# Selective attention and a gated FFN in one kernel: k's DMA transposes write the matmul operands directly, and the seven-product down projection also serves token tile 1

## The chip, the core and the metric

The kernel runs on one core of one Trainium2 chip. TensorE (PE) multiplies matrices, VectorE (DVE), ScalarE (ACT) and GpSimd (POOL) work on elements, and SyncE (SP) here only issues DMAs. The engines have their own instruction streams, run in program order each, and wait for one another by semaphores. The metric is the device time in microseconds (us); the time before is the median of three runs, 375.34 us (374.61 to 375.9).

## The reference

```python
scores = (q @ k.T) / sqrt(64)                      # 8 batches x 8 heads, 576 x 576, head size 64
cum    = cumsum(maximum(s, 0))
scores = where(causal, -1e9, scores + minimum(-(cum_i - cum_j), 0))
attn   = softmax(scores) @ v                       # -> x, 4608 tokens x 512
g, val = x @ w_gate, x @ w_val                     # 512 -> 1536
out    = (silu(g) * val) @ w_out                   # 1536 -> 512, float32
```

## The kernel before

**Attention.** The 64 heads (called kk, batch-major) go in 16 groups hb of four heads. For each head `score_piece` (line 338) makes the causal half of the transposed scores in four chunks ci = 0 to 3: each takes a PSUM bank, PE multiplies (line 359), ACT takes the exponential into `pt` (line 369) and the bank is free again. POOL masks the diagonal blocks of chunks 0 and 3 (lines 374, 379). `av_piece` (line 386) multiplies by v and a column of ones (line 396), `av_out` (line 404) divides by the sum on DVE (lines 412, 413). There are eight PSUM banks, handed out in the order in which they were given back, so a new use of a bank waits for whoever read it last.

**The operand tiles.** `KQ[hb % 2][r]` (line 91) serves heads 2r and 2r+1 of a group. It has 128 rows and two planes, 0 for q and 1 for k. Rows 64r to 64r+63 hold the 64 features, transposed, of the two heads side by side (2 x 576 = 1152 columns, `NR * S`). The first four rows of the other half hold the bias (parts of the cumulative sums in bf16, made once in `HL`), the rest of that half zeros, so that one 128-row matmul gives q.k plus bias. `aug` (line 178) writes the bias rows of a group with four DMAs from POOL's queue (line 183).

**How q and k get there.** `load_qk` brings 576 KB each for a group into `raw` (line 140), `cast_one` makes bf16. Groups 0 to 4 are transposed on PE. Groups 5 to 15 (`NPE = 5`) go through DRAM: `scratch` (line 258) writes them out, `transposes` (line 267) issues one DMA transpose each for k and q into a 128 x 1152 tile `pk` or `pq`, whose rows are the two heads pairs' features one above the other, and `split` (line 272) copies each half, 64 x 1152, to its `KQ` tile on DVE (line 274): four copies a group. `pk` and `pq` have one buffer each.

**What sets the order.** `attn_items` (line 547) is a generator that emits heads in order; after every chunk it calls `side(h, step, ci)` (line 467), where h is the group in work, step the head in it. `side` is a timetable by hand:

- `load_qk(h + 3)` at (0,1), on SP;
- for group h + 2: casts on ACT early in the group, `scratch` at (2,0), `transposes` at (3,0) (group 6: (3,0) and (3,3)), all DMAs on SP;
- for group h + 1: `aug` at (0,1) on POOL; `split` of k and of q appended to a list `later` at ci = 1 of step 0 and step 1 (groups 5 to 7: steps 1 and 2). Group 5 has its scratch and transposes here, at (0,1) and (0,3).

SP's queue also carries the loads of v and `x_in` (line 434): finished heads go in pairs from POOL (`x_out`, line 430) to a DRAM scratch `xs`, and SP transposes them into the FFN's input `XT` (line 437), which it can do only when `xs` has landed.

**The FFN.** Nine tiles of 512 tokens. `gate_value` (line 644) makes 12 pairs of 128 x 512 products (line 629), tanh on ACT (line 650) and two DVE instructions (lines 652, 663) for each. Then comes the down projection. `down_plain` (line 678) is 48 matmuls of 512 columns (line 686). `down_seven` (line 713) splits the product in 2 x 2 blocks and makes it from seven block products m1 to m7 of 12 matmuls of 256 columns each, 84 in all (line 735). It needs sums of the activations (`su`, lines 670, 671; differences in place, line 672), sums and differences of the weights made once (`weight_op`, line 603: six sums into `WS`, four differences in place in `WO`), and some additions of the outputs (lines 774, 794, 800, 852). Tiles from `FIRST7 = 2` on use `down_seven`, tiles 0 and 1 `down_plain`.

**The interleaving.** The main loop (line 1003) runs through the FFN's items of each tile (about one unit of cost per 512-column quadruple) and calls `pump` to emit attention up to a position, so that both share PE; attention is about four heads and a tile ahead. After each item it may call `do_later(1)`: in the gate stage after every fourth item (in tile 1 every second), in the down stage after every item. That is where the copies enter DVE's stream. All that is left in `later` is emitted at step 0 of the next group.

Of the kernel before, what the change touches and what calls it, by code (L numbers as in the profile page):

```python
# [13 lines left out]
BF16 = mybir.dt.bfloat16  # L14
# [5 lines left out]
def kernel(  # L20
# [11 lines left out]
    nc = tc.nc  # L32
    PSUM = bass.MemoryType.PSUM

    B, H, S, D = q.shape
# [7 lines left out]
    NR = HB // 2  # L43
# [20 lines left out]
    def pt_col(tj, bi):  # L64
# [6 lines left out]
    cp = ctx.enter_context(tc.tile_pool(name="cp", bufs=2))  # L71
# [8 lines left out]
    NPE = 5  # L80
    XB = 2
    KS = {i: dram.tile([NR * S, 128], BF16, name=f"ks{i}") for i in range(NPE, NHB)}
# [3 lines left out]
    QS = {i: dram.tile([NR * S, 128], BF16, name=f"qs{i}") for i in range(NPE, NHB)}  # L86
# [4 lines left out]
    KQ = [  # L91
        [const.tile([128, 2, NR * S + 64], BF16, name=f"kq{e}{i}") for e in range(2)]
        for i in range(2)
    ]
# [9 lines left out]
    first = first_sbuf.enter_context(tc.tile_pool(name="first", bufs=1))  # L104
# [5 lines left out]
    with tc.manual_schedule():  # L110
        loaded = {}
        SRC = {"q": (q, 0), "k": (k, 1)}
# [13 lines left out]
        def give(b):  # L126
            clock[0] += 1
            released[b] = clock[0]
# [18 lines left out]
        def load_qk(hb):  # L147
            load_one(hb, "k")
            load_one(hb, "q")

        def load_v(b, cs, eng=nc.sync):
            if 0 in cs:
                loaded["v", b] = raw.tile([128, NCH, H, D], FP32, tag="rawv", bufs=1, name="rawv")
            t = loaded["v", b]
            for c in cs:
                n = 128 if c < 4 else TAIL
                eng.dma_start(
                    t[0:n, c, :, :],
                    v[b, :, c * 128 : c * 128 + n, :].rearrange("h p d -> p h d"),
                )  # L160

        def cast_v(b, c, eng):
            n = 128 if c < 4 else TAIL
            dst, src_t = VT[b % 2][0:n, c, :, 0:D], loaded["v", b][0:n, c, :, :]
            if eng is nc.scalar:
                nc.scalar.copy(dst, src_t)
            else:
                eng.tensor_copy(dst, src_t)  # L168
# [89 lines left out]
        def scratch(hb):  # L258
            for name, SC in (("k", KS), ("q", QS)):
                nc.sync.dma_start(  # L260
                    SC[hb].rearrange("(x j) c -> x (j c)", j=J),
                    cts[name, hb].rearrange("x j r d -> x (j r d)"),
                )

        prs = {}

        def transposes(hb):
            for name, SC in (("k", KS), ("q", QS)):
                prs[name, hb] = cp.tile([128, NR * S], BF16, tag="p" + name, bufs=1, name="p" + name)
                nc.sync.dma_start_transpose(prs[name, hb], SC[hb])  # L270

        def split(hb, name, r):
            kq = SRC[name][1]
            nc.vector.tensor_copy(
                KQ[hb % 2][r][64 * r : 64 * r + 64, kq, 0 : NR * S],
                prs[name, hb][64 * r : 64 * r + 64, :],
            )

        tps = {}
# [175 lines left out]
        later = []  # L455

        def do_later(n):
            while n > 0 and later:
                f, *args = later.pop(0)
                f(*args)  # L460
                n -= 1
# [5 lines left out]
        def side(h, step, ci):  # L467
            bh = HB * h + step
            for c in V1_AT.get((bh, ci), ()):
                cast_v(1, c, nc.gpsimd)  # L470
            if bh == H + 4 and ci == 3:
                load_v(2, range(5))
            if h == 4 and (step, ci) in ((0, 1), (2, 1)):
                load_qk(6 + step // 2)
            if h >= 5 and h + 3 < NHB and (step, ci) == (0, 1):
                load_qk(h + 3)
            hb = h + 1
            if NPE <= hb < NHB:
                late = hb == NPE
                if late and (step, ci) == (0, 1):  # L480
                    scratch(hb)
                if late and (step, ci) == (0, 3):
                    transposes(hb)
                if (step, ci) == (0, 1):
                    aug(hb, GP4)
                first = 1 if hb < NPE + 3 else 0
                if step in (first, first + 1) and ci == (3 if late else 1):
                    for r in range(NR):
                        later.append((split, hb, "kq"[step - first], r))
            hb = h + 2  # L490
            if hb == NPE and step == 3 and ci % 2 == 1:
                cast_one(hb, "kq"[ci // 2], nc.gpsimd)
            if NPE < hb < NHB:
                six = hb == NPE + 1
                if (step, ci) == ((2, 0) if six else (0, 2)):
                    cast_one(hb, "k", nc.scalar)
                if (step, ci) == ((2, 2) if six else (1, 2)):
                    cast_one(hb, "q", nc.scalar)
                if (step, ci) == ((3, 0) if six else (2, 0)):
                    scratch(hb)  # L500
                if (step, ci) == (3, 3 if six else 0):
                    do_later(NR * 2)
                    transposes(hb)
            if ci != 1:
                return
            bn = h // 2 + 1
            if 3 <= bn < B:
                if h % 2 == 0:
                    if step == 2:
                        load_v(bn, (0, 1))  # L510
                    if step == 3:
                        load_v(bn, (2, 3, 4))
# [34 lines left out]
        def attn_items():  # L547
            for kk in range(H, BH + 2):
                h, step = divmod(kk, HB)
                if kk < BH:  # L550
                    if step == 0:
                        do_later(NR * 2)
                    if step == 1 and 3 < h + 1 < NPE:
                        cast_one(h + 1, "k", nc.gpsimd)
                        cast_one(h + 1, "q", nc.gpsimd)
                    if step == 2 and 3 < h + 1 < NPE:
                        aug(h + 1, GP4)
                    for ci in range(4):
                        score_piece(kk, ci)
                        side(h, step, ci)  # L560
                        side_v(h, step, ci)
                        yield kk + 0.1 + ci / 8
                        if (step, ci) in PREP_AT.get(h, ()):
                            prep_one(
                                h + 1, PREP_AT[h][step, ci],
                                (nc.scalar, nc.vector)[ci // 2] if h == 2 else None,
                            )
                            yield kk + 0.1 + ci / 8
                for x in X_AT.get(kk, (kk - 2,)):
                    if x % 2 == 1 and H <= x < BH:  # L570
                        if x < XB * H:
                            x_pe(x // 2)
                            yield kk + 0.5
                        else:
                            x_in(x // 2)
                for p in AV_AT.get(kk, (kk - 1,)):
                    if H <= p < BH:
                        av_piece(p, (0, 1, 2))
                        yield kk + 0.6
                        av_piece(p, (3,))  # L580
                        yield kk + 0.7
                        av_piece(p, (4,))
                        av_out(p)
                        if p >= XB * H and p % 2 == 1:
                            x_out(p // 2)
                        yield kk + 0.8

        stores = []
        FIRST7 = 2
        HD = DM // 2  # L590
        HT = TT // 2
        NP = NFT // 2
# [51 lines left out]
        def gate_value(tt, hps, sus):  # L644
            xt = XT[:, :, (tt % 3) * TT : (tt % 3 + 1) * TT]
            for ft in range(NFT):
# [20 lines left out]
                give(vbs)  # L667
                if k2 == 1 and tt >= FIRST7:
                    su = PTP[0].tile([128, 3, HT], BF16, tag="su", bufs=NP, name="su")
# [200 lines left out]
        def ffn_items(tt):  # L870
            hps, sus = [], []
            flush()
            yield from gate_value(tt, hps, sus)
            if tt < FIRST7:
                yield from down_plain(tt, hps)
# [111 lines left out]
                except StopIteration:  # L987
                    state["pos"] = 1e9

        W_SUMS = [(j, i) for i in range(3) for j in range(2)]  # L990
        W_DIFFS = [(j, i) for i in (3, 4) for j in range(2)]
        LAGS = [0, 1.65] + [3.6] * NTT
        hook = {n: [] for n in range(1, 37)}
# [9 lines left out]
        for tt in range(NTT):  # L1003
            lo = H * (tt + 1) + LAGS[tt]
            hi = min(H * (tt + 2) + LAGS[tt + 1], BH + 2)
            span = 36 if tt < FIRST7 else 34.5
            if hi == BH + 2:
                span = 30
            n0 = 5 if tt == 0 else 0
            n = 0  # L1010
            todo = {FIRST7 - 1: W_SUMS, FIRST7: W_DIFFS}.get(tt, [])
            if tt == FIRST7:
                for _ in range(3):
                    weight_op(*todo.pop(0))
            for i, cost in enumerate(ffn_items(tt)):
                n += cost
                if todo and (i >= 24 if tt < FIRST7 else i % 2 == 1):
                    weight_op(*todo.pop(0))
# [46 lines left out]
```

## Time and profile before

| | before |
|---|---|
| median of 3 runs | 375.34 us (374.61 to 375.9) |
| profiled execution: time | 376.97 us |
| profiled execution: span of its instructions | 375.3 us |
| PE busy | 364.6 us (97%) |
| DVE busy | 290.4 us (77%) |
| ACT busy | 240.6 us (64%) |
| POOL busy | 212.2 us (57%) |
| gate and value matmuls (line 629) | 864 |
| plain down matmuls (line 686), block products (line 735) | 96, 588 |
| DMA | 64.23 MB in 97147 packets, of these 77233 under 512 B |
| SP's queue, POOL's queue: share of 16 engines | 45.3%, 22.6% |

The profile gives each group of instructions by line with its busy time, its mean duration and the idle time of its engine just before it; the stage tables give busy time by stretch of the span; the timeline lists instructions with start and duration, and in brackets what ended an idle time. Two further readings are used: the marks that the trace holds of when a DMA has landed (updates of its semaphore), and the program order, which says for each PSUM bank who freed it and when PE next used it. A matmul's own duration includes its way through the array, so rates are read from start to start. In the profile the tiles' gate stages begin at 77.05 (tile 1), 119.84 (tile 2), 158.89 (tile 3) and then every 39.06 us to tile 6.

### The profile page before, as it was taken

Reading aid. Unit: us, or ns where it says so; the run is one execution under the profiler, and the core shown is the slowest. Engines: PE = TensorE matmul, PEld = TensorE weight load, DVE = VectorE, ACT = ScalarE, POOL = GpSimd, SP = SyncE. Lnnn points to the kernel's source line nnn. Section 1 sums busy time; section 2 is a strip of 40 time slices with the busy share of each in tenths; the row PEclk is TensorE's granted clock in tenths of the full one; section 3 lists DMA queues with packets and bytes.
Section 4 is the critical chain, followed back from the end, with each engine's and each line's share of the span. In section 5 each row is a group of like instructions: output and inputs, shape, how many; then the busy total and the mean of one; then the engine's idle time right before and its main releaser. Section 6 shows DMA issues by size and latency. Waiting matters only on the chain.

```text
span 375.3 us, 8799 instructions
## 1 busy us (share of the span) xinstructions
PE 364.6 (97%) x3300; PEld 231.7 (62%) x3300; DVE 290.4 (77%) x578; ACT 240.6 (64%) x471; POOL 212.2 (57%) x325
## 2 busy tenths in 40 slices
PE   7799999999999999999999999999999999999995
PEld 6575556655555556855685558655865585476464
DVE  7777877458995999679976997599858867975984
ACT  8597687598976887578757876687465523323321
POOL 8973556765465647494649555955675416315320
PEclk9899999999999999999999999999999999999999
DMA  7899999899778986896769665995132103002003
GB/s 237 200 263 265 186 256 275 224 312 242 228 197 233 264 237 189 169 291 213 206 157 263 174 161 166 263 184 161 39 110 72 35 19 127 2 0 92 23 0 114
DMA packets 97147, 64.23 MB, mean 171 GB/s; under 512 B 77233, under 2 KB 82737, under 8 KB 97105
## 3 DMA queue, kind: packets, MB, share of 16 engines
q1 hardware_dynamic: 84976, 41.46, 45.3%
q0 software_dynamic: 12128, 22.21, 22.6%
q8 instruction: 26, 0.43, 0.5%
q14 instruction: 17, 0.13, 0.1%
HBM read 37.90 MB, written 19.86 MB: 154 GB/s over the span
## 4 chain that ended last, share of the span: by engine, by line
PE 90%; POOL 3%; DVE 2%; ACT 1%; DMA 1%; issue 1%; DVEq 0%; POOLq 0%; ACTq 0%
PE bank L629 47%; PE bank L735 17%; PE bank L359 11%; PE bank L396 8%; PE bank L686 6%; DMA kq<-HL 1%; ACT pt L369 1%; DVE kq L316 1%; DVE pp L652 1%; PE bank L287 1%; PE bank L353 1%; POOL vt L168 1%; PE bank L445 1%; DVE ht L663 1%; ACT th L650 0%
## 5 line engine op out<-in xcount | busy, mean ns | idle before, releaser
L369 ACT ACTIVATE pt<-bank 128x512 bf16<-128x512 f32 (+1 forms) x256 | 120.6, 508 | 31.5 <-PE bank L359 18.9
L629 PE MATMUL bank<-XT,wg 128*128 128x512 bf16 x432 | 111.4, 379 | 0.4 <-DVE pp L652 0.3
L629 PE MATMUL bank<-XT,wv 128*128 128x512 bf16 x432 | 110.9, 379 | 0.1
L650 ACT ACTIVATE th<-bank 128x512 bf16<-128x512 f32 x108 | 64.7, 599 | 56.1 <-PE bank L629 51.4
L652 DVE SCALAR_TENSOR_TENSOR pp<-th,bank 128x512 bf16<-128x512 bf16 x108 | 73.7, 682 | 18.7 <-ACT th L650 18.2
L663 DVE SCALAR_TENSOR_TENSOR ht<-pp,bank 128x512 bf16<-128x512 bf16 x108 | 74.1, 686 | 10.3
L359 PE MATMUL bank<-kq 128*128 128x128 bf16 (+4 forms) x576 | 76.9, 243 | 2.5 <-DMA kq<-HL 2.0
L672 POOL TENSOR_TENSOR ht<-ht 128x512 bf16<-128x512 bf16 x35 | 40.4, 1154 | 52.3 <-DVE su L670 52.2
L359 PEld LDWEIGHTS <-kq 128*128 128x128 bf16 x576 | 46.6, 99 | 33.5 <-issue 2.8
L629 PEld LDWEIGHTS <-wv 128*128 128x128 bf16 x432 | 38.3, 98 | 36.3 <-issue 0.2
L629 PEld LDWEIGHTS <-wg 128*128 128x128 bf16 x432 | 38.3, 98 | 34.2 <-issue 0.7
L374 POOL TENSOR_SCALAR_AFFINE_SELECT pt<-pt 128x512 bf16<-128x512 bf16 x56 | 36.8, 657 | 30.0 <-ACT pt L369 22.8
L396 PEld LDWEIGHTS <-pt 128*128 128x128 bf16 x960 | 41.8, 98 | 17.1
L396 PE MATMUL bank<-vt,pt 128*128 128x65 bf16 x960 | 46.7, 194 | 0.1
L430 POOL DMA_DIRECT2D xs<-ot x24 | 21.7, 904 | 30.2 <-DVE ot L413 27.8
L735 PEld LDWEIGHTS <-ht 128*128 128x128 bf16 x336 | 31.1, 98 | 4.3
L413 DVE TENSOR_TENSOR ot<-bank,rc 128x320 bf16<-128x320 f32 x64 | 31.5, 491 | 2.2
L183 POOL DMA_DIRECT2D kq<-HL x48 | 28.9, 605 | 0.0
L686 PE MATMUL bank<-wo,ht 128*128 128x512 bf16 x96 | 25.8, 379 | 0.0
L735 PEld LDWEIGHTS <-su 128*128 128x128 bf16 x252 | 23.5, 98 | 3.3
L379 POOL TENSOR_SCALAR_AFFINE_SELECT pt<-pt 128x64 bf16<-128x64 bf16 x56 | 14.8, 264 | 16.3 <-ACT pt L369 16.1
L800 POOL TENSOR_TENSOR ysb<-ysb 128x512 f32<-128x512 f32 x12 | 15.2, 1270 | 15.3 <-DVE ysb L794 15.3
(93 smaller groups left out, 387.2 us busy)
## 6 DMA issues: line engine op xcount, KB each, us to landing
out_dram<-ysb POOLq DMA_DIRECT2D x32, 256.0 KB, 4.0
rawv<-in_v_dram SPq DMA_DIRECT2D x28, 256.0 KB
rawk<-in_k_dram SPq DMA_DIRECT2D x12, 576.0 KB
rawq<-in_q_dram SPq DMA_DIRECT2D x12, 576.0 KB
xs<-ot POOLq DMA_DIRECT2D x24, 160.0 KB, 3.8
ks<-ck SPq DMA_DIRECT2D x11, 288.0 KB
qs<-cq SPq DMA_DIRECT2D x11, 288.0 KB
rawk<-in_k_dram POOLq DMA_DIRECT2D x3, 576.0 KB, 7.6
```

What stands on the lines that cost most here:

```text
L359: nc.tensor.matmul(sc[:, o : o + w], T[:, 1, e * S + 128 * tj : e * S + 128 * (tj + 1)], T[:, 0, e * S + lo : e * S + hi], start=not maske ...
L369: nc.scalar.activation(pt[:, c0 : c0 + n], sc, AF.Exp, scale=0.125)
L374: nc.gpsimd.affine_select(pt[:, 1088:1600], pt[:, 1088:1600], pattern=[[0, 4], [1, 128]], compare_op=ALU.is_ge, fill=zreg, base=0, channel ...
L396: nc.tensor.matmul(av[:, bi * (D + 1) : (bi + 1) * (D + 1)], pt[:, c0 : c0 + 128], VT[b % 2][:, tj, h, :], start=(tj == 0), stop=(tj == bi),)
L413: nc.vector.tensor_mul(ot[:, :, e * D : (e + 1) * D], av3[:, :, 0:D], rc[:, :, None].to_broadcast([128, NCH, D]),)
L629: nc.tensor.matmul(view(bs, TT), w[:, c, f0 : f0 + 128], xt[:, c, :], start=(c == 0), stop=(c == 3),)
L650: nc.scalar.activation(th, pg, AF.Tanh, scale=0.5)
L652: nc.vector.scalar_tensor_tensor(pp, in0=th, scalar=1.0, in1=pg, op0=ALU.add, op1=ALU.mult)
L663: nc.vector.scalar_tensor_tensor(hp[:, 2 * k2 : 2 * k2 + 2, :].rearrange("p a n -> p (a n)"), in0=pp, scalar=0.5, in1=pv, op0=ALU.mult, op ...
L672: (nc.vector if ft == NFT - 1 else nc.gpsimd).tensor_sub(hp[:, 1:3, :], hp[:, 1:4:2, :], hp[:, 0:3:2, :])
L686: nc.tensor.matmul(view(pys[ts_], DM), hps[ft // 2][:, 2 * (ft % 2) + half, c0 : c0 + 128], WO[j][:, ft % WKO, :], start=(ft == 0), stop=( ...
L735: nc.tensor.matmul(ps, lhs(p), rhs(p), start=(first and p == 0), stop=(last and p == NP - 1), skip_group_check=True,)
```

## The change

Three things change together.

- `transposes` issues three DMA transposes a group instead of two: k's whole 128 x 1152 transpose once into each of the two `KQ` tiles (plane 1), q's into `pq` as before. In each `KQ` tile the half that is not its own gets the other pair's k; its first four rows are then overwritten by `aug`, and the others meet zeros in q's plane. `split` copies only q: two copies a group.
- The timetable moves. For groups 6 to 15 `transposes` goes from (3,0) (group 6: (3,3)) of the group two back to (0,1) of the group before, after `load_qk`; `aug` goes from (0,1) to (2,1), since it has to follow the transposes; q's copies are appended at (1,3). Group 5 keeps its transposes at (0,3), with its copies at (2,1).
- `FIRST7` becomes 1, so tile 1 uses `down_seven`; the weight sums are made in tile 0's down projection, in the order of the halves of `w_out`, and the differences in tile 1's gate stage.

```diff
         def transposes(hb):
-            for name, SC in (("k", KS), ("q", QS)):
-                prs[name, hb] = cp.tile([128, NR * S], BF16, tag="p" + name, bufs=1, name="p" + name)
-                nc.sync.dma_start_transpose(prs[name, hb], SC[hb])
-
-        def split(hb, name, r):
-            kq = SRC[name][1]
+            for r in range(NR):
+                nc.sync.dma_start_transpose(KQ[hb % 2][r][:, 1, 0 : NR * S], KS[hb])
+            prs[hb] = cp.tile([128, NR * S], BF16, tag="pq", bufs=1, name="pq")
+            nc.sync.dma_start_transpose(prs[hb], QS[hb])
+
+        def split(hb, r):
             nc.vector.tensor_copy(
-                KQ[hb % 2][r][64 * r : 64 * r + 64, kq, 0 : NR * S],
-                prs[name, hb][64 * r : 64 * r + 64, :],
+                KQ[hb % 2][r][64 * r : 64 * r + 64, 0, 0 : NR * S],
+                prs[hb][64 * r : 64 * r + 64, :],
             )
...
                 late = hb == NPE
                 if late and (step, ci) == (0, 1):
                     scratch(hb)
-                if late and (step, ci) == (0, 3):
+                if (step, ci) == (0, 3 if late else 1):
                     transposes(hb)
-                if (step, ci) == (0, 1):
+                if (step, ci) == (2, 1):
                     aug(hb, GP4)
-                first = 1 if hb < NPE + 3 else 0
-                if step in (first, first + 1) and ci == (3 if late else 1):
+                if (step, ci) == ((2, 1) if late else (1, 3)):
                     for r in range(NR):
-                        later.append((split, hb, "kq"[step - first], r))
+                        later.append((split, hb, r))
...
-                if (step, ci) == (3, 3 if six else 0):
-                    do_later(NR * 2)
-                    transposes(hb)
...
                     if step == 0:
-                        do_later(NR * 2)
+                        do_later(NR)
...
-        FIRST7 = 2
+        FIRST7 = 1
...
-        W_SUMS = [(j, i) for i in range(3) for j in range(2)]
+        W_SUMS = [(j, i) for j in range(2) for i in range(3)]
```

## The prediction

> **What bounds the kernel now.** I read the page's busy shares, then the busy time by stage, the chain in order of time, and last the timelines of SP, VectorE (DVE) and TensorE (PE) around one group of heads. The stages (busy us of PE, PEld, DVE, ACT, POOL; granted clock; DMA share; GB/s):
>
> ```profile
> 118.00:147.00 29.00, 29.00 (x250) 16.07 (x248) 25.48 (x51) 23.06 (x46) 17.73 (x27) 1.00 0.97 240
> 158.00:186.00 28.00, 28.00 (x245) 15.87 (x244) 23.59 (x48) 22.30 (x44) 19.54 (x30) 1.00 0.84 219
> ```
>
> PE has no gap from about 57 us on. Start to start, a 512-column matmul takes 0.216 us and a 256-column one 0.109 us, and this holds in mixed stages too. The chain shows both in tile 7, where attention is over:
>
> ```profile
> 302.25 9.17 PE bank L735 x84
> 311.43 20.72 PE bank L629 x96
> ```
>
> So the time is PE's work plus PE's stalls: PE work removed is a gain, a stall is a loss that nothing later gives back, and other engines count only through PE's stalls.
>
> **Part 1, tile 1 by seven products.** Out go 48 matmuls of 512 columns, 48 x 0.216 = 10.37 us; in come 84 of 256, 9.17 us (row above). Gain: **1.2 us** of PE, 0.3% of the time, about what a measurement of this kernel can tell from no change. DVE gets the sums of tile 1: 6 x (0.43 + 0.28) = 4.3 us, a subtraction (0.4), the four weight differences earlier (2.6), and loses six k copies (6 x 0.64 = 3.9): 3.4 us more in a stage where it was busy 22.85 of 27 us. Tile 2 (first row above) carries the same kinds of work beside gapless PE, so I cost this, POOL's five 1.15-us subtractions and two of 1.27 us at nothing; without that cover it would be up to 3 us. The six weight sums (4.1 us) move into tile 0's down projection, where DVE is busy 11.3 of 21 us: nothing.
>
> **Part 2, k's copies.** 22 DVE copies go:
>
> ```profile
> L274 DVE COPY kq<-pk 64x1152 bf16<-64x1152 bf16 x22 | 14.1, 643 | 0.3
> ```
>
> That is 14.1 us of an engine that is not the bound: no time by itself, only slack. The idle column matters more: 0.3 us in 22 copies, so DVE never waited for a transpose. The price is 11 more DMA transposes: 11 x 1.25 us of SP's issue time, and 1152 packets of 256 B each, which took 1.2 us when alone (177.76 to 178.95).
>
> **Part 3, the order.** This decides. For groups 6 to 15 the transposes were issued at step (3,0) (group 6: (3,3)) of the group two back, and k's first copy ran 7 to 12 us after that (87.44 to 95.05, 155.81 to 167.26), q's later still. Now they are issued at (0,1) of the group before, *behind* load_qk(h+3) and the x_in before it, and q's copy is queued at (1,3). Take group 11. SP in the trace of before:
>
> ```profile
> 181.65 1.13 SPq L437 DMA_TRANSPOSE XT<-xs  x1
> 182.83 0.57 SPq L140 DMA_DIRECT2D rawk<-in_k_dram  x1
> 183.45 0.46 SPq L140 DMA_DIRECT2D rawq<-in_q_dram  x1
> ```
>
> The x_in can't come sooner: SP waits for xs to land, the largest row of SP's waits:
>
> ```profile
> SPq L437 <- DMA xs<-ot: 93.9, 17, 9.6
> ```
>
> The two loads (1.18 MB) are issued at 182.83; their packets run until 188.2, and the last landing mark is at 189.64 (in ten such pairs the mark comes 5.7 to 7.3 us after the first issue). Transposes issued behind a load have always landed behind it: at 119.67, behind v, pk landed after 6.4 us, against 2.9 us when nothing was ahead (176.52). Three now follow the loads: 188.2 + 3 x 1.2 + 0.5 from last packet to mark (178.95 to 179.43) = 192.3; I take 9.7 us after the load's issue, 192.5.
>
> The Trainium skill, "DMA: Bandwidth & Descriptors", section "Queues, rings and completion order", says that on each DMA engine the descriptors of one queue are consumed in ring order, which speaks against this place for the transposes and agrees with that landing. Its fit in "Anatomy of one DMA" (2.0 us plus bytes over 436 GB/s, given for the POOL path) would put the pair at 4.7 us, an estimate, where the trace has 6.8; by it q would land 2.1 us earlier and the eight losses below would be some 10 us less.
>
> When does DVE reach q's first copy? In program order it comes after tile 3's item 26, behind the last subtraction:
>
> ```profile
> 188.76 0.42 DVE L672 TENSOR_TENSOR ht<-ht 128x512 bf16<-128x512 bf16 x1
> 189.21 0.77 DVE L274 COPY kq<-pk 64x1152 bf16<-64x1152 bf16 x1
> 190.01 0.92 DVE L274 COPY kq<-pq 64x1152 bf16<-64x1152 bf16 x2
> 190.97 0.20 DVE L412 RECIPROCAL rc<-bank 128x5 f32<-128x5 f32 x1
> 191.20 0.49 DVE L413 TENSOR_TENSOR ot<-bank,rc 128x320 bf16<-128x320 f32 x1
> 191.60 0.41 DVE L852 TENSOR_TENSOR de<-s,bank 128x256 f32<-128x256 f32 x1
> ```
>
> It reaches it at 189.2 and waits till 192.5. Behind it are the second copy, an av_out and L852: 2.0 us (190.01 to 192.01), so L852 ends at 194.5. L852 must be done before PE's m5 overwrites its bank:
>
> ```profile
> 192.68 0.82 PE L735 MATMUL bank<-wo,su 128*128 128x256 bf16 x6
> ```
>
> So PE stalls about 194.55 - 192.68 = 1.9 us. The same reckoning for each group, in the times of before. "Load": issue of load k, or where it moves to once the transposes ahead of x_in are gone (landing of xs plus 1.2 us per x_in piece). "PE": the first use of PE that hangs on DVE work behind the copy; "behind": that work.
>
> ```
> group   load    q lands (+9.7)   behind   PE's use     stall
> 6       92.5    102.2            1.85      98.38        5.7
> 7      107.3    117.0            (wait 4.0 less 2.4 of bank cover)  1.6
> 8      124.6    134.3            1.15     134.31        1.1
> 9      143.3    153.0            2.05     153.63        1.4
> 10     162.5    172.2            1.15     173.36        0.0
> 11     182.8    192.5            2.05     192.68        1.9
> 12     203.5    213.2            1.15     212.42        1.9
> 13     222.9    232.6            2.05     231.74        2.9
> ```
>
> In group 7 DVE reaches the copy near 113.0 (tile 3's m1 puts it 7 us after its gate stage); 2.4 us is the usual time between an engine's freeing a bank and PE's next use of it in that stage. Groups 14 and 15 have no load ahead and group 5 had none: no wait. Sum: 16.5 us. The bias rows' DMAs (POOL, four per group) now wait for k's transposes too: POOL may stand up to 3 us with masks and x_out queued behind it, but at the same moments as DVE, and the rows still have 4 us or more before their first score (landing 1.9 to 5.7 us after issue). I add nothing.
>
> **Sum.** -1.2 + 16.5 = +15.3 us. The profiled execution (376.97 us, span 375.3) becomes 392.3; it ran 1.6 us above the median of 375.34, which becomes **390.6 us**.
>
> The unseen cost is the landing of three transposes behind two loads. Low end: if only SP's issue counted (1.1 + 3 x 1.3 + 2 us = 7.0 after the load's issue), every row above loses 2.7 us, only groups 6 and 13 stall (3.0 and 0.2), and the time is 375.34 + 3.2 - 1.2 = 377.3. High end: 11.0, as when each transpose lands 1.5 us or more behind the last (pk 1.5 to 3.0 us behind the load ahead of it in other rows); each row gains 1.3 us, the sum is 26.8, the time 401. I take 9.7 because it is group 11's own packets, with little else on the queues.
>
> **Rivals.** (a) *Faster:* q's transposes land before DVE needs them, or the banks cover the wait. Then only part 1 counts: 374.1 us, perhaps a little less with DVE relieved. It decides from about 7 us between load and landing. For it: DVE loses 14 us of copies, so banks come free sooner; against it: groups 6, 9, 11 and 13 would need a landing before their own loads are down. (b) *The middle:* transposes held up by SP's issue alone, 377.3 us. (c) *Within 0.3%:* the wait is covered nearly everywhere and the first stall (group 6) eats the 1.2 us: about 375. (d) *Part 1 gives nothing* because tile 1 becomes bound by DVE: 1.2 us more on the forecast, 391.8.
>
> **How the numbers follow.** Forecast with (b) and (d), slower: 0.83. (a) 0.13, (c) 0.04. Range 376.5 to 401: it leaves out (a), (c) and a few hundredths above, and takes in both ends of the landing.
>
> **What would show it.** L735 has 672 matmuls, L686 48; the DVE copies are 22, all from pq, and they now have idle time ahead of them that a DMA pq<-qs ended, longest in group 6 (near 95 us) and least in 14 and 15; PE gaps of 1 to 6 us follow each, eight in all; SP shows two loads and then three transposes in a row. It is wrong if the copies wait for nothing (the transposes overtake the loads or land faster), if they wait but PE shows no gap (banks deeper than I read), or if POOL's wait ahead of the bias rows ends last at a score matmul.

## The result and the profile after

| | before | after |
|---|---|---|
| median, runs of the comparison | 374.98 us (374.07 to 377.17, 6 runs) | 414.37 us (413.66 to 417.92, 6 runs) |
| ratio to before | | 1.1066 (95%: 1.103 to 1.1102) |
| profiled execution: time, span | 376.97, 375.3 us | 414.15, 412.4 us |
| PE gaps over 0.3 us from 57 us on, summed | 0 | 29.3 us |
| PE at half the granted clock, from 57 us to the last few us | 0 | 27.3 us |
| k's DMA transposes (into `pk`, into the operands), median issue on SP | 1.31 us | 2.36 us |

The change costs 39.4 us; 390.6 was forecast, at most 401. A few executions of a kernel run some per cent slower than its others, and the ratios leave them out. In the changed file lines from L629 on are four lower (L629 is L625, L652 is L648, L735 is L731, L852 is L848); those up to L437 are the same. The experiments' edits shift lines too: in e5 and e9 L361, L381 and L398 are L359, L379 and L396, in e9 L632 is L625 (L629 before), and in e12 L402, L419 and L635 are L396, L413 and L629.

The page of the changed kernel, its totals and its 40 slices (tenths busy):

```profile
span 412.4 us, 8951 instructions
...
PE 376.1 (91%) x3336; PEld 240.2 (58%) x3336; DVE 291.8 (71%) x575; ACT 241.0 (58%) x471; POOL 222.2 (54%) x332
...
PE   8898998977697979998899949899999999999996
...
PEclk9999999999598998999899979999999999999999
```

PE was busy 364.6 of 375.3 us and is now busy *longer* in a longer span, though it has less to do: the clock row drops in slices where PE's row does, or in the slice behind. By stage (busy PE, PEld, DVE, ACT, POOL; clock; DMA share; GB/s), two stretches with the same kind of work as the two that the prediction shows, and one around the deepest drop:

```profile
99.90:113.00 13.10, 6.67 (x35) 3.27 (x34) 6.72 (x13) 3.81 (x9) 4.52 (x7) 0.61 0.62 149
126.00:155.00 29.00, 23.70 (x208) 15.08 (x207) 16.39 (x35) 16.67 (x34) 17.56 (x28) 0.92 0.91 224
168.00:197.00 29.00, 25.82 (x251) 17.72 (x250) 16.90 (x37) 19.50 (x39) 18.95 (x30) 1.00 0.96 235
```

DVE had 25.48 and 23.59 us of work in such stretches and now has 16.4 and 16.9. It is not short of time: it stands. Where attention is over, nothing has changed; the chain has tile 7's stages at the same lengths:

```profile
339.53 9.17 PE bank L731 x84
348.70 20.72 PE bank L625 x96
```

What DVE stands for is in its group of copies and in the waits (us in total, times, longest):

```profile
L274 DVE COPY kq<-pq 64x1152 bf16<-64x1152 bf16 x22 | 12.2, 553 | 29.4 <-DMA pq<-qs 29.2
```

```profile
DVE kq L274 <- DMA pq<-qs: 29.2, 9, 5.9
...
POOL kq L183 <- DMA kq<-ks: 7.9, 4, 4.1
```

One case from issue to clock, group 10. SP (start, duration):

```profile
183.39 0.58 SPq L140 DMA_DIRECT2D rawk<-in_k_dram  x1
184.03 0.48 SPq L140 DMA_DIRECT2D rawq<-in_q_dram  x1
184.67 7.61 SPq L269 DMA_TRANSPOSE kq<-ks  x2
192.38 1.29 SPq L271 DMA_TRANSPOSE pq<-qs  x1
```

Two loads, then three transposes, as forecast, but k's two transposes took SP 7.6 us to issue instead of 2.6 (two at the 1.3 of before). The profile puts these holds down to PE's scores; the scores that read this tile had ended at 179.5, so that is only the nearest event. q lands at 196.2. DVE, which comes to the copy at 192.5:

```profile
196.22 0.45 DVE L274 COPY kq<-pq 64x1152 bf16<-64x1152 bf16 x1 [3.68 <-DMA pq<-qs]
...
196.81 0.49 DVE L413 TENSOR_TENSOR ot<-bank,rc 128x320 bf16<-128x320 f32 x1
```

And PE, whose next `av` needs the bank that this L413 reads:

```profile
197.35 0.46 PE L396 MATMUL bank<-vt,pt 128*128 128x65 bf16 x10 [3.16 <-DVE ot L413]
...
199.56 1.91 PE L625 MATMUL bank<-XT,wg 128*128 128x512 bf16 x4
...
202.72 1.03 PE L625 MATMUL bank<-XT,wg 128*128 128x512 bf16 x4
```

The gap, 3.3 us from start to start, is nearly as long as DVE's wait of 3.7. After it the same four matmuls take 1.91 us and then 1.03 again: from 198.2 to 201.6 the granted clock is one half.

**Where 37.1 us of span come from.** Gaps 29.3 (24.2 behind q's copies, 4.4 in tiles 0 and 1 between 65 and 92 us, some small ones); half clock 10.4 (the excess of the matmuls' pitch over the usual in those stretches); seven products in tile 1, -1.2; the time before 57 us was 2.0 us shorter in this execution; the remaining 0.6 is spread.

### The profile page after: what moved, and what is told of

The parts are those of the page before. It is cut to its first block, busy times and chain, and to the rows that moved or that the text cites. A ratio compares the mean times of both kernels' runs of the same rounds, so it can differ in the third digit from the quotient of the medians.

```text
span 412.4 us, 8951 instructions
## 1 busy us (share of the span) xinstructions
PE 376.1 (91%) x3336; PEld 240.2 (58%) x3336; DVE 291.8 (71%) x575; ACT 241.0 (58%) x471; POOL 222.2 (54%) x332
## 4 chain that ended last, share of the span: by engine, by line
PE 66%; DVE 12%; DMA 9%; issue 5%; ACT 4%; POOL 2%; SPq 1%; DVEq 0%; ACTq 0%; POOLq 0%
PE bank L625 38%; PE bank L731 12%; PE bank L359 8%; DMA pq<-qs 7%; PE bank L396 6%; DMA kq<-HL 3%; DVE pp L648 3%; DVE ot L413 2%; ACT pt L369 2%; DVE ht L659 2%; PE bank L682 1%; ACT th L646 1%; DVE kq L274 1%; DVE kq L316 1%; DVE rc L412 1%
## 5 line engine op out<-in xcount | busy, mean ns | idle before, releaser
L625 PE MATMUL bank<-XT,wg 128*128 128x512 bf16 x432 | 114.9, 388 | 3.1 <-DVE ot L413 2.7
L625 PE MATMUL bank<-XT,wv 128*128 128x512 bf16 x432 | 114.3, 388 | 0.3
L648 DVE SCALAR_TENSOR_TENSOR pp<-th,bank 128x512 bf16<-128x512 bf16 x108 | 73.8, 683 | 26.4 <-ACT th L646 26.1
L359 PE MATMUL bank<-kq 128*128 128x128 bf16 (+4 forms) x576 | 77.3, 243 | 7.2 <-DVE ot L413 5.6
L668 POOL TENSOR_TENSOR ht<-ht 128x512 bf16<-128x512 bf16 x40 | 46.1, 1152 | 58.5 <-DVE su L666 54.4
L359 PEld LDWEIGHTS <-kq 128*128 128x128 bf16 x576 | 46.7, 99 | 31.8 <-issue 4.2
L396 PEld LDWEIGHTS <-pt 128*128 128x128 bf16 x960 | 43.2, 100 | 35.9 <-issue 21.4
L396 PE MATMUL bank<-vt,pt 128*128 128x65 bf16 x960 | 47.8, 196 | 17.7 <-DVE ot L413 10.7
L625 PEld LDWEIGHTS <-wv 128*128 128x128 bf16 x432 | 39.5, 100 | 39.2 <-issue 5.1
L625 PEld LDWEIGHTS <-wg 128*128 128x128 bf16 x432 | 39.4, 100 | 38.2 <-issue 5.6
L731 PEld LDWEIGHTS <-ht 128*128 128x128 bf16 x384 | 35.7, 99 | 5.0
L413 DVE TENSOR_TENSOR ot<-bank,rc 128x320 bf16<-128x320 f32 x64 | 31.5, 492 | 2.2
L274 DVE COPY kq<-pq 64x1152 bf16<-64x1152 bf16 x22 | 12.2, 553 | 29.4 <-DMA pq<-qs 29.2
L731 PEld LDWEIGHTS <-su 128*128 128x128 bf16 x288 | 27.2, 99 | 9.4 <-issue 5.5
L796 POOL TENSOR_TENSOR ysb<-ysb 128x512 f32<-128x512 f32 x14 | 17.6, 1268 | 18.0 <-DVE ysb L790 14.9
L731 PE MATMUL bank<-WS,ht 128*128 128x256 bf16 x192 | 26.8, 277 | 0.0
```

The lines of the kernel that those rows point to most:

```text
L359: nc.tensor.matmul(sc[:, o : o + w], T[:, 1, e * S + 128 * tj : e * S + 128 * (tj + 1)], T[:, 0, e * S + lo : e * S + hi], start=not maske ...
L396: nc.tensor.matmul(av[:, bi * (D + 1) : (bi + 1) * (D + 1)], pt[:, c0 : c0 + 128], VT[b % 2][:, tj, h, :], start=(tj == 0), stop=(tj == bi),)
L413: nc.vector.tensor_mul(ot[:, :, e * D : (e + 1) * D], av3[:, :, 0:D], rc[:, :, None].to_broadcast([128, NCH, D]),)
L625: nc.tensor.matmul(view(bs, TT), w[:, c, f0 : f0 + 128], xt[:, c, :], start=(c == 0), stop=(c == 3),)
L648: nc.vector.scalar_tensor_tensor(pp, in0=th, scalar=1.0, in1=pg, op0=ALU.add, op1=ALU.mult)
L668: (nc.vector if ft == NFT - 1 else nc.gpsimd).tensor_sub(hp[:, 1:3, :], hp[:, 1:4:2, :], hp[:, 0:3:2, :])
```

## The experiments

Each is the kernel before or after with the edit shown. Unless a single run is said, the ratio is to runs of the kernel before from the same session, with its 95% interval.

**The two parts alone.** `e1_part1_only` is the kernel before with

```diff
-        FIRST7 = 2
+        FIRST7 = 1
-        W_SUMS = [(j, i) for i in range(3) for j in range(2)]
+        W_SUMS = [(j, i) for j in range(2) for i in range(3)]
```

`e2_part2_only` is the kernel after with the same lines turned back.

> The kernel before with tile 1's down projection by seven products alone. The prediction's reading (its cost on DVE is covered): 1.2 us less than before, 373.8. The rival, from the profile after, where PE stood 1.3 us at 66 us and 2.2 us at 84 us with DVE busy on weight sums and differences: 1 to 3 us more than before, 376 to 378, with those two gaps in its trace and none from a DMA of pq.

> The changed kernel with tile 1 by the plain product again, so the direct transposes and the new timetable alone. Theory (DVE waits for q's transposes, PE stalls, and PE's clock is granted at half after the longer stalls): 35 to 38 us more than before, 410 to 413, with 25 to 30 us of DVE idle ahead of the copies. Rival (tile 1's new load on DVE is what makes the waits hurt): under 15 us more.

Measured: part 1 alone 380.32 us, 1.0142 (1.0117 to 1.0167); part 2 alone 411.08 us, 1.0946 (1.0899 to 1.0994). Part 2 is the loss, with a time as its theory gave it (DVE's idle time of 32.6 us is above the theory's 25 to 30), but part 1, forecast at -1.2, costs 5, more than the rival's 1 to 3 too. In e1's tile 1 DVE (first fence) and PE (second):

```profile
76.25 2.06 DVE L615 TENSOR_TENSOR wo<-wo 128x768 bf16<-128x768 bf16 x2
78.23 1.23 DVE L619 TENSOR_TENSOR wo<-wo 128x768 bf16<-128x768 bf16 x1
```

```profile
85.99 1.17 PE L629 MATMUL bank<-XT,wg 128*128 128x512 bf16 x4 [2.51 <-DVE ot L413]
```

The three weight differences ahead of the gate stage take 3.3 us where before, at tile 2, two of them took 0.56 to 0.99 us each. PE has a gap of 2.7 us at 83.3, one of 1.3 us at 65.4 beside the weight sums in tile 0, two of 0.4 and 0.5, and one half-clock stretch of 3.4 us.

**What makes part 1's cost.** `e10_part1_spread` is e1 with the sums late in tile 0 and one difference after every fourth item of tile 1; `e15_part1_diffs_apart` puts them two items further (`i % 4 == 1`); `e13_part1_no_diffs` is e10 with `W_DIFFS = []`: it leaves the differences out, and the block products use the plain halves of `w_out`.

```diff
-            if tt == FIRST7:
-                for _ in range(3):
-                    weight_op(*todo.pop(0))
...
-                if todo and (i >= 24 if tt < FIRST7 else i % 2 == 1):
+                if todo and (i >= 33 if tt < FIRST7 else i % 4 == 3):
```

> The kernel before with tile 1 by seven products, the weight sums after item 33 of tile 0 instead of 24, and the four differences one after each fourth item of tile 1 instead of three at its start. Theory (the 6.6 us that part 1 lost were DVE's weight work ahead of PE's banks): the gaps at 65 and 83 us go, and the time is 373.5 to 375.5, the 1.2 us of PE gained or nearly. Rival (the sums of tile 1's activations, which stay, are what DVE can't carry there): 377 and more.

> Part 1 alone as in e10, but the four weight differences are left out altogether, so the block products of all tiles use the plain halves of w_out (that part of the computation is changed). Theory (the differences, each 1.5 to 2.1 us on DVE beside POOL's subtraction, make PE's gaps in tile 1): the gaps of 2.61 us at 82.00 and 2.14 at 90.00 and the four of 0.4 to 0.6 us after 98 go; the 8.75 us of stalls fall below 2 and the time to 374 to 377. Rival (the su work with the ten heads is what DVE cannot carry): stalls of 4 us or more remain, 378 to 381.

> Part 1 alone as in e10, with each weight difference two items away from the su pair and POOL's subtraction. Theory (they cost so much for being beside POOL's subtraction): each takes 0.6 to 1.2 us instead of 1.5 to 2.1, gaps below 1.3 us, 376 to 378.5. Rival (DVE has no room for them wherever they stand): gaps of 2 us and more remain, 380 to 382.

Measured: e10 1.0184 (1.0165 to 1.0203), e13 1.0105 (1.0067 to 1.0143), e15 1.0109 (1.0074 to 1.0145). Spreading did not help, and the time is in the rival's range: the gap at 65 us went, but each difference now stands right behind a `su` pair and takes 1.5 to 2.1 us. In e15, away from them, they take 0.55 to 0.99 us, so that part of e15's theory holds; the profiled execution took 381.87 us, but its interval does not tell it from e13, and gaps of 2.1 and 1.2 us stay, so neither of its expectations holds whole. e13, with no differences at all, is the telling one: 3.8 us of gaps remain (8.2 in e10), between its two expectations, and the time is in its rival's range. DVE, POOL and PE at its largest gap:

```profile
81.19 0.42 DVE L670 TENSOR_TENSOR su<-ht 128x512 bf16<-128x512 bf16 x1
...
81.83 1.33 DVE L274 COPY kq<-pk 64x1152 bf16<-64x1152 bf16 x1
```

```profile
81.70 1.15 POOL L672 TENSOR_TENSOR ht<-ht 128x512 bf16<-128x512 bf16 x1 [1.71 <-DVE su L670]
```

```profile
83.97 1.02 PE L629 MATMUL bank<-XT,wg 128*128 128x512 bf16 x4 [1.88 <-DVE ot L413]
```

The `su` pair takes 0.7 us of DVE, and POOL's subtraction, which it starts, ends at 82.85; DVE's copy, 0.44 us at the least, ends 0.3 us after that. e1 has the same copy of 1.33 us ahead of its gap, at 83.86. The Trainium skill, "SBUF — State Buffer", section "Who interferes with whom", says that DVE copies in a two-port mode, and two-input instructions against a POOL instruction that reads SBUF, share one port pair with POOL as an exclusive lock: who comes second waits for the other's whole instruction. The traces agree that the second waits. Over all traces of this case 25 of these copies began 0.02 to 0.84 us into a POOL subtraction: they took 1.47 down to 0.62 us, the less the later they began, and all ended 0.31 to 0.34 us behind its end, so a copy's end is set by POOL's. (Those that began later still ended 0.33 to 0.57 us behind.) e10's difference of 1.53 us from 81.83 ends 0.42 us behind its subtraction (81.79 to 82.94). That a shared port is the reason is the page's; and no run here takes the subtraction away, so what this wait costs in time is argued and not shown.

**Which wait makes part 2's cost.** `e3_loads_behind`, the kernel after with the loads issued behind the transposes:

```diff
-            if h >= 5 and h + 3 < NHB and (step, ci) == (0, 1):
-                load_qk(h + 3)
...
                     transposes(hb)
+                if h >= 5 and h + 3 < NHB and (step, ci) == (0, 1):
+                    load_qk(h + 3)
```

`e4_copies_late`, the kernel after with q's copies appended four chunks later: `(2, 3)` instead of `(1, 3)`. `e5_q_early`, the kernel after with q's transpose where it was in the kernel before, `(3, 0)` of the group two back (group 6: `(3, 3)`), behind a `do_later(NR)`; k's two stay at (0,1).

> The changed kernel with the two loads of group h + 3 issued behind the three transposes at (0,1) instead of ahead of them; the same transposes, the same copies at the same places. Theory (the place in SP's queue makes q late): q lands some 6 us after SP reaches the first transpose instead of 9.5 to 13.4 after the load, DVE's idle time ahead of the copies falls from 29 us to under 6, and the time to 378 to 385. Rival (the third transpose and the writes into the operands themselves are slow): it stays above 400.

> The changed kernel with q's copies of groups 6 to 15 appended at (2,3) instead of (1,3), one head later in DVE's stream; every DMA stays where it is. Theory (what costs is DVE standing in front of a late transpose): idle ahead of the copies under 4 us, no stretch of half clock in the attention stages, 377 to 383 us. Rival (late k transposes and the bias rows behind them hold PE at the next group's first scores, whatever DVE does): above 395, with PE waiting at the scores for a DMA of kq.

> The changed kernel with q's transpose back at its old place, (3,0) of the group two back, where pq is free; k's two transposes stay at (0,1) behind the loads. Theory: the copies never wait for DMA, and the time is 375 to 380. Rival (k's two transposes are what comes late): bias rows and scores wait, above 390.

Measured: e3 1.0446 (1.0386 to 1.0505), e4 1.0379 (1.0351 to 1.0406), e5 1.0345 (1.03 to 1.039). Each takes away more than half of the loss, and none all of it: all three are slower than their theories gave and faster than their rivals. The waits, in the order e3, e4, e5, one fence each:

```profile
DVE kq L274 <- DMA pq<-qs: 15.2, 8, 3.0
```

```profile
POOL kq L183 <- DMA kq<-ks: 13.0, 8, 4.4
...
DVE kq L274 <- DMA pq<-qs: 10.0, 4, 3.9
```

```profile
POOL kq L183 <- DMA kq<-ks: 29.9, 8, 7.3
```

In e3 k's transposes issue at 1.30 us in the median instead of 2.36, and DVE's wait halves. They are, after and in e3 (ns, least, median and most):

```profile
L269 SPq DMA_TRANSPOSE kq<-ks x22: 1184/2355/5107, 72.1 to 299.0; - x22
```

```profile
L269 SPq DMA_TRANSPOSE kq<-ks x22: 1184/1298/4482, 71.6 to 279.3; - x22
```

In e5 DVE never waits for q, and POOL takes its place: it stands at the bias rows for k's transposes, with the diagonal masks queued behind. POOL and PE around 144 us of e5:

```profile
143.87 2.40 POOL L183 DMA_DIRECT2D kq<-HL  x4 [7.29 <-DMA kq<-ks]
...
147.40 0.24 POOL L381 TENSOR_SCALAR_AFFINE_SELECT pt<-pt 128x64 bf16<-128x64 bf16 x1
```

```profile
147.70 0.27 PE L398 MATMUL bank<-vt,pt 128*128 128x65 bf16 x3 [3.62 <-POOL pt L381]
```

So the change has two waits one behind the other, and the shorter is hidden by the longer.

**Both waits mended, and the third transpose.** `e9_part2_mended` joins e3 and e5 for part 2 alone: q's transpose early, k's two at (0,1) ahead of the loads. `e11_both_mended` is that with e10's part 1. `e6_third_alone` is the kernel before plus one more transpose of k a group into a tile that nothing reads. `e14_e9_no_third` is e9 with `range(1)` for k in groups 6 to 15, so heads 2 and 3 of those groups meet an old k.

> Part 2 alone (tile 1 by the plain product), with q's transpose at its old place, (3,0) of the group two back, and k's two at (0,1) ahead of the loads. Theory (the whole loss of part 2 is waiting for late transposes, DVE at q's copies and POOL at the bias rows): neither engine waits for a transpose for more than 3 us in all, and the time is within 1% of before, 374 to 379. Rival (direct writes by the transposes cost by themselves, by their traffic or by writing the operands): 385 and more, as with q early alone.

> Both mended parts together: k's direct transposes at (0,1) ahead of the loads, q's at its old place, tile 1 by seven products with its weight work spread. Theory: the sum of the two, 373 to 377. Rival (what was gained on DVE by leaving out k's copies now pays): 372 or less.

> The kernel before with a third transpose for each of groups 5 to 15, of k into a spare tile that nobody reads, behind the first one. It prices the added DMA and SP's issue by themselves. Theory (the DMA is cheap, its place is dear): within 2 us of before, 374 to 377. Rival (the transposes' own traffic slows the rest): over 385.

> The kernel of e9 without the second of k's two direct transposes in groups 6 to 15, so that heads 2 and 3 of those groups are scored with an old k (that part of the computation is changed); two transposes a group as in the kernel before. Theory (what is left of part 2's cost in e9 is the third transpose's time on the queue): POOL's wait for k's transposes falls from 8.7 us to below 4, the waits of 2.0 us for bias rows and 1.7 us for XT go, 375 to 377. Rival (the later place of k's transposes and of the bias rows costs it whatever their number): 380 or more with waits of the same kind.

Measured: e9 1.0192 (1.0149 to 1.0234), e11 1.0191 (1.0169 to 1.0213), e6 1.0098 (1.0067 to 1.0129), e14 1.0095 (1.0069 to 1.0121). From 36 us the two mends bring part 2 to 7. The third transpose on its own costs 3.7 us, more than e6's theory of 2 and far less than its rival; without it e9's 7.2 fall to 3.6. e9 itself lies between its theory (374 to 379) and its rival (385), and e11 above both of its own. e11 loses 7.2 us where its halves lose 7.2 (e9) and 6.9 (e10); they do not add up, and why is open. So e6 and e14 put about half of what stays in e9 down to one more transpose a group; that the other half is the later place of k's transposes is argued, not tested by itself. In e9 the loss reaches PE mainly at two spots, at the bias rows, which wait for k's transposes, and at the FFN's input, which SP issues behind them:

```profile
105.36 0.40 PE L361 MATMUL bank<-kq 128*128 128x128 bf16 x4 [2.01 <-DMA kq<-HL]
...
123.39 0.38 PE L632 MATMUL bank<-XT,wg 128*128 128x512 bf16 x1 [1.67 <-DMA XT<-xs]
```

e14 fell between its theory (375 to 377 expected, 378.8 measured) and its rival (380 or more). No version made here is faster than the kernel before.

**What a wait on DVE costs PE.** In the kernel before, k's second copy is made again, so that DVE is held and nothing else moves: `e7_dve_held_6` and `e8_dve_held_12` six and twelve times more in groups 10 and 12, `e12_dve_held_2_to_5` two to five times more in groups 8, 10, 12 and 14. The added copies start 0.49 us apart, so DVE is held 2.96 and 5.91 us, and 0.99, 1.48, 1.97 and 2.46 us, somewhat more than the expectations reckon by the copies' own 0.457 us. All three are single runs.

```diff
+            if name == "k" and r == 1:
+                for _ in range({8: 2, 10: 3, 12: 4, 14: 5}.get(hb, 0)):
+                    nc.vector.tensor_copy(
...
```

> The kernel before with k's second copy of groups 10 and 12 made six times more, the same data to the same place, so DVE is held some 2.7 us at two places of the gate stage. If a stall of PE costs only itself: each place costs 1 to 2 us, 377 to 379 in all. If PE's clock is halved for a while after a stall: PE's granted clock shows stretches of 0.5 there only if the stall is long; I expect none at this length.

> The same with twelve copies more, DVE held some 5.4 us at two places. If a stall costs only itself: 4 us a place, 383 in all. If the clock is granted at half after a long stall: a stretch of 3.4 to 6.8 us at 0.5 behind each, in which 512-column matmuls start every 0.427 us, and 1.7 to 3.4 us more a place, 386 to 390 in all.

> The kernel before with k's second copy made 2, 3, 4 and 5 times more in groups 8, 10, 12 and 14: DVE held 0.9, 1.35, 1.8 and 2.25 us at the same place of four tiles. If the banks cover 1 us there, the first stalls nothing and the others 0.3 to 1.3 us; if they cover 0.2 us, as with 2.7 us held, PE stalls 0.7, 1.1, 1.6 and 2.0 us. Half clock behind the last one or two only. Time 380 to 384.

Measured: 382.72, 389.78 and 382.4 us; e7 is above its 377 to 379, the others are as expected. PE's gaps are 2.75 us twice (e7) and 5.70 us twice (e8). In e12, the first gap, the matmuls behind the third, and the last gap with the matmuls behind it (the idle time in the brackets is counted from the end of the matmul before, through the array):

```profile
132.79 0.46 PE L402 MATMUL bank<-vt,pt 128*128 128x65 bf16 x10 [0.66 <-DVE ot L419]
...
214.22 1.03 PE L635 MATMUL bank<-XT,wv 128*128 128x512 bf16 x4
...
255.23 0.46 PE L402 MATMUL bank<-vt,pt 128*128 128x65 bf16 x10 [2.09 <-DVE ot L419]
255.53 1.84 PE L635 MATMUL bank<-XT,wv 128*128 128x512 bf16 x4
```

Start to start the four gaps are 0.82, 1.27, 1.76 and 2.25 us: PE loses what DVE is held, less 0.2 us, in all three. Behind the last one the four matmuls take 1.84 us, at half clock, and the same happens behind both gaps of e7, where none was expected, and of e8; behind 1.76 us they take 1.03.

## Why the prediction was wrong

**The mechanism was right.** The copies from `pq` wait, longest in group 6, least in 14 and 15; SP shows two loads and three transposes in a row; a PE gap follows each of the eight long waits. The table sets the forecast's rows beside the trace of after (us); the forecast's waits, where its text does not state them, follow from its landing and the time at which DVE is done with what stands ahead of the copy in the trace of before.

| group | q lands after load k's issue (9.7 forecast) | DVE's wait: forecast, measured | PE's stall: forecast, measured |
|---|---|---|---|
| 6 | 10.2 | 7.1, 5.9 | 5.7, 6.4 |
| 7 | 11.0 | 4.0, 3.2 | 1.6, 3.2 |
| 8 | 11.3 | 1.5, 2.7 | 1.1, 2.4 |
| 9 | 10.0 | 2.9, 1.9 | 1.4, 0.7 |
| 10 | 12.8 | 0.3, 3.7 | 0.0, 3.3 |
| 11 | 9.5 | 3.3, 1.9 | 1.9, 0.6 |
| 12 | 13.2 | 2.3, 5.8 | 1.9, 5.4 |
| 13 | 11.5 | 4.4, 3.4 | 2.9, 2.2 |
| sum | mean 11.2 | 25.8, 28.5 | 16.5, 24.2 |

**Step that was mis-sized: "I take 9.7 us after the load's issue".** Group 11, from which it was taken, landed at 9.5; the mean is 11.2, and groups 10 and 12 took 12.8 and 13.2 (v loads were issued ahead of both, but ahead of 6 and 8 too, so they alone do not explain it). "11 x 1.25 us of SP's issue time" was right only with nothing in the way: 1.30 and 1.26 us in the median where the transposes precede the loads (e3, e9), 2.3 to 2.4 where they follow them (after, e4, e5). The high end's 11.0 with its 26.8 us of stalls was nearer to the measured 11.2 with 24.2. Yet the waits that came of it were only 2.7 us longer in all (28.5 for 25.8), since DVE, too, came to the copies later. A smaller slip: for a landing 2.1 us earlier the forecast's own rows lose some 12 us, not 10.

**Step that failed: "2.4 of bank cover".** The forecast made 16.5 us of stalls out of its waits, 9.3 less than they come to; measured are 24.2, only 4.3 less. In group 7 the stall equals the wait. In all five groups whose copy falls in a gate stage (6, 7, 8, 10, 12) waits of 21.3 us gave stalls of 20.7; e12 shows the same, but for 0.2 us, from a hold of 1 us on. Only in the down stage (9, 11, 13) PE lost about 1.2 us less than DVE waited. The low end, and rival (a) in part, rested on a cover that is not there. Landing and cover together are worth 7.7 us, of which some 5 are the cover.

**Step that was missing: the clock.** The sum was PE's work plus PE's stalls at one rate. The trace of before had no stall in this part, so it showed no price for one beyond its length. Half clock adds 10.4 us in after, and e7, e8 and e12, where only DVE is held, show that a stall brings it on. By itself this term would have put the forecast at 401.0, the end of the range; with the terms before and behind it the time reaches 414.

**Step that failed: part 1 "at nothing", beside gapless PE as in tile 2.** The 1.2 us of PE are there, but tile 1 has 4.4 us of gaps in its place and before it (5.2 us of loss in e1). Tile 1 carries about ten heads, tile 2 eight, and DVE's 4.2 us of room there was read as an average; what ends last is one chain, `su` pair, copy and L413, and there the 0.7 us and a copy lengthened to 1.33 us show at once (read from e1's and e13's rows, not tested apart). Even the forecast's price without cover (3 us) was too low. That the six weight sums cost nothing was wrong too (1.3 us at 65 us in e1).

**POOL's wait, "I add nothing".** This held in after (7.9 us of waits, at the same moments as DVE's), but only because DVE's wait is longer: e5 shows it worth several us as soon as DVE's is gone.

**The sum again.** 392.3 forecast for the profiled execution + 7.7 (landing and cover) + 4.4 (tiles 0 and 1) + 10.4 (clock) = 414.8; less the 2.0 us before 57 us, and with 1.3 of small terms, 414.1; it took 414.15. Of the rivals, (a), (b) and (c) are excluded by the waits; (d), tile 1 bound by DVE, came nearest to part 1 and was priced at 1.2 where e1 has 6.4 (-1.2 forecast, +5.2 measured).

**Open.** Why SP's issue of a transpose lengthens behind loads; why q landed later in groups 10 and 12; what the later place costs by itself (e14 loses 3.6 us, with PE's waits for bias rows of 2.5 us and for `XT` of 1.1 us in its profile); and whether tile 1's chain would hold with POOL's subtraction elsewhere.

## What to carry to other kernels

When a copy is replaced by a transfer that writes the operand itself, the transfer cannot start until the operand's last reader is done; ask what stands ahead of it on its queue at that later moment, and which in-order engine will stand at the first instruction that needs it, with what behind. A wait that is taken away may uncover a shorter one right behind it, so follow all readers of the new transfer before pricing the first. On a gapless PE count a stall at its length, and from about 2.2 us on also the slower clock that may follow it, and give an engine's "room" in a stage no credit where one short chain sets the pace.

## What the hardware showed that was not expected

**Half clock after short stalls.** The half-clock stretches come in lengths of 3.4, 6.8 and 10.2 us, in which a 512-column matmul takes 0.427 us instead of 0.216, so that each 3.4 us full of PE's work costs 1.7. Over all traces of this case such a stretch came in none of 4 PE gaps of 1.6 to 1.9 us, in 12 of 26 gaps of 2.0 to 3.3 us (at 2.25 us in e12, not at 2.66 us in e11), and in all 9 gaps longer than that. The Trainium skill, "TensorE: Matmul & The Clock Gate", section "Part 1: The HAM clock gate (the "warmup" mystery)", gives a free-running window of 3413 ns and the half clock after at least one idle window. The lengths agree. So does the free-running window: in each trace all half-clock stretches begin on one grid of 3.413 us, whatever the gaps do, and this grid tells which of the 26 gaps brought one. Take every step of it from 57 us to near the end that ran at full clock, 1542 in the 17 traces, and add up PE's idle time in it (start to start, gaps over 0.1 us): half clock followed each of the 21 steps with 2.17 us or more and none of the others, which had 2.14 us at the most. So a gap costs the clock when enough of it falls into one step. That a whole idle window is needed does not agree, and the measurement decides.

**A transpose's issue depends on what is ahead.** For k's, 1.3 us in the median with loads behind (e3, e9), 2.3 to 2.4 with loads ahead (after, e4, e5), 5.1 at the most. In e6 one more of them a group costs 3.7 us though nothing reads it.

**DVE beside POOL.** The same 64 x 1152 copy took 0.44 to 0.46 us in most places and 1.33 to 1.47 where it began with POOL's 1.15-us subtraction, and a 128 x 768 weight difference 0.55 against 1.5 to 2.1.
